# The head of a fused attention and MLP block: x tile 1 through ScalarE's queue, its statistics beside a square root, its transposes inside the first V group, tile 3 transposed by DMA

## Chip, cores, metric

One core of one Trainium2 chip. The metric is the device time of one execution in microseconds (us). "Before" and "changed" name the two kernels.

## The reference

A pre-normalized block: sliding-window attention, then a SiLU MLP, both with a residual, for one sequence of 2048 tokens with 1024 channels.

```python
h  = x + attention(layernorm(x), wqkv, wo)      # 32 heads of 32, window 256
h2 = h + silu(layernorm(h) @ w1) @ w2           # F = 3584
# x [1,2048,1024], wqkv [1024,3072], all bfloat16
# layernorm: (x - mean) / sqrt(var + 1e-5), no weights
```

Only the first 25 us matter here: the first 512 tokens ("block 0", four tiles of 128) are loaded, normalized, transposed, and multiplied by wv, then by the q and k columns of wqkv.

## The kernel before

The loads at the start, all from SP's queue (`wv` is the last third of wqkv, in two halves of 1 MB; each x tile has 256 KB):

```python
load_x(0, 0)
load_wqkv(2 * D)             # wv, first half
load_x(0, 1)
load_wqkv(2 * D + 512)       # wv, second half
load_x(0, 2)
load_x(0, 3)
for c0 in (0, D, 512, D + 512):
    load_wqkv(c0)            # q and k columns
```

Normalization of a tile and its transpose for block 0. VectorE takes the statistics, ScalarE the square root, TensorE transposes into PSUM, ScalarE copies to SBUF:

```python
def ln_first(xt, st, rs, j):
    ln_stats(xt, st, j)                                   # VectorE: 2 bn_stats, 1 bn_aggr
    nc.scalar.activation(out=rs[:, j:j + 1], in_=st[:, j, 1:2], func=ACT.Sqrt, bias=eps[:], scale=1.0)
    nc.vector.reciprocal(out=rs[:, j:j + 1], in_=rs[:, j:j + 1])
    for h in range(2):
        ln_norm(xt[:, h * 512:(h + 1) * 512], st, rs, j)  # VectorE

def turn_first(xt, dst, j):
    for h in range(2):
        ...                                               # four TensorE transposes
        nc.scalar.copy(...)                               # PSUM -> SBUF
```

The order of block 0. `v_group(0, j, c)` is eight matmuls of 128x128 by 128x512 for tile j and half c of wv; `qk_group` the same for 128 columns of q or k and all four tiles:

```python
ln_first(x_ring[0], st, rs, 0)
turn_first(x_ring[0], lnT_b[0], 0)
ln_first(x_ring[1], st, rs, 1)
v_group(0, 0, 0, act)
turn_first(x_ring[1], lnT_b[0], 1)
ln_first(x_ring[2], st, rs, 2)
v_group(0, 1, 0, act)
v_group(0, 0, 1, act)
turn_first(x_ring[2], lnT_b[0], 2)
ln_first(x_ring[3], st, rs, 3)
v_group(0, 1, 1, act)
v_group(0, 2, 0, act)
turn_first(x_ring[3], lnT_b[0], 3)
v_group(0, 2, 1, act)
dummy = small.tile([P, 1], F32, name="dummy", tag="dummy")   # pool "small": two buffers
nc.scalar.activation(out=dummy[:], in_=eps[:], func=ACT.Exp) # draws the table load forward
v_group(0, 3, 0, act)
v_group(0, 3, 1, act)
...
for g in range(G):                                           # G = 8
    qk_group(0, 0, g, act)
    qk_group(0, 1, g, dve)
    ...
```

The softmax here doesn't subtract the row's maximum and nothing guards it: scores larger than these inputs give would overflow.

## Time and profile before

| | before |
|---|---|
| time, median of 3 (range) | 698.12 us (698.09 to 698.29) |
| span of the profile | 696.4 us |
| TensorE busy | 99% |
| first q/k group starts in the chain | 24.22 us |

The chain of waits is read from the end of the program backwards; where it names TensorE without a break, only less TensorE work or an earlier start can shorten the time. The prediction shows its head, the timeline and the DMA rate.

### The profile page before, as it was taken

How to read it: one execution, taken by the hardware profiler on the slowest of the kernel's cores; microseconds unless marked ns; L12 is line 12 of the kernel's file. 1: busy time of each engine (PE TensorE's matmuls, PEld its weight loads, DVE VectorE, ACT ScalarE, POOL GpSimd, SP SyncE). 2: the span in 40 equal slices, each digit the busy share in tenths (PEclk: the TensorE clock that was granted, in tenths of full speed). 3: DMA queues.
4: the chain of work that ended last, by engine and by line, in shares of the span. 5: the costliest groups of instructions: out<-in, count | busy, mean ns of one | idle time of the engine just before them, and what ended most of it. 6: DMA issues, size and time to landing. Idle time of an engine off the chain costs nothing.

```text
span 696.4 us, 12339 instructions
## 1 busy us (share of the span) xinstructions
PE 690.6 (99%) x5099; PEld 332.1 (48%) x5099; DVE 288.1 (41%) x608; ACT 258.5 (37%) x323; POOL 175.2 (25%) x391
## 2 busy tenths in 40 slices
PE   8999999999999999999999999999999999999998
PEld 3444444555555555544444444444444444444445
DVE  5347645743444448543315234433133251233111
ACT  4316667777777777621310023300033200233000
POOL 1006676777777777600000000000000000000000
PEclk9999999999999999999999999999999999999999
DMA  9541142036331678891123510023300024100010
GB/s 312 171 65 66 25 86 68 17 54 176 92 122 24 190 257 262 203 315 40 32 75 99 106 38 1 1 78 81 84 0 1 10 94 93 45 1 1 30 39 24
DMA packets 75400, 60.57 MB, mean 87 GB/s; under 512 B 49232, under 2 KB 59472, under 8 KB 75344
## 3 DMA queue, kind: packets, MB, share of 16 engines
q1 hardware_dynamic: 75344, 59.78, 30.8%
q8 instruction: 40, 0.66, 0.4%
q14 instruction: 16, 0.13, 0.1%
HBM read 39.85 MB, written 8.39 MB: 69 GB/s over the span
## 4 chain that ended last, share of the span: by engine, by line
PE 98%; DMA 1%; DVE 0%; ACT 0%; SPq 0%; issue 0%
PE hacc L540 19%; PE hacc L577 17%; PE acc L240 16%; PE acc L577 10%; PE acc L540 9%; PE acc L230 8%; PE acc L259 7%; PE o_ps L331 4%; PE sc L277 3%; PE hacc L259 1%; PE o_ps L346 1%; PE sc L305 1%; DMA r_o<-in_A_x_dram 1%; PE o_ps L208 0%; DVE ln_st L170 0%; ACT r_w L209 0%
## 5 line engine op out<-in xcount | busy, mean ns | idle before, releaser
L322 POOL TENSOR_SCALAR_AFFINE_SELECT r_e<-r_e 128x256 bf16<-128x256 bf16 (+1 forms) x384 | 172.3, 479 | 116.7 <-ACT r_e L314 65.9
L285 ACT ACTIVATE r_e<-sc 128x1024 bf16<-128x1024 f32 x144 | 139.5, 1021 | 45.1 <-PE sc L277 31.0
L577 PEld LDWEIGHTS <-r_a 128*128 128x128 bf16 x952 | 90.9, 98 | 103.0
L540 PEld LDWEIGHTS <-r_w 128*128 128x128 bf16 x896 | 87.3, 98 | 104.8
L577 PE MATMUL hacc<-r_a 128*128 128x512 bf16 (+2 forms) x616 | 122.5, 360 | 0.0
L540 PE MATMUL hacc<-r_e,r_w 128*128 128x512 bf16 x456 | 100.9, 379 | 0.0
L549 ACT ACTIVATE r_n<-hacc 128x512 f32<-128x512 f32 x30 | 17.9, 597 | 178.9 <-PE hacc L540 178.9
L577 PE MATMUL acc<-r_a 128*128 128x512 bf16 x336 | 74.0, 379 | 0.0
L240 PEld LDWEIGHTS <-r_w 128*128 128x128 bf16 x512 | 46.5, 98 | 57.0 <-issue 7.0
L242 DVE CAST r_a<-acc 128x512 bf16<-128x512 f32 x56 | 38.7, 690 | 73.1 <-PE acc L240 56.5
L240 PE MATMUL acc<-r_t,r_w 128*128 128x512 bf16 x256 | 60.0, 379 | 0.0
L240 PE MATMUL acc<-r_w 128*128 128x512 bf16 x256 | 58.2, 380 | 0.0
L259 PE MATMUL acc<-r_o,r_a 128*128 128x512 bf16 x208 | 49.4, 380 | 0.0
L540 PE MATMUL acc<-r_e,r_w 128*128 128x512 bf16 x216 | 49.1, 379 | 0.0
L331 PEld LDWEIGHTS <-r_e 128*128 128x128 bf16 x1152 | 39.6, 96 | 17.0
L314 ACT ACTIVATE r_e<-sc 128x1024 bf16<-128x1024 f32 x36 | 34.9, 1021 | 21.2 <-PE sc L305 20.1
L331 PE MATMUL o_ps<-r_a,r_e 128*128 128x33 bf16 x1152 | 40.2, 178 | 0.0
L592 DVE SCALAR_TENSOR_TENSOR r_t<-hacc,r_t 128x512 bf16<-128x512 f32 (+2 forms) x22 | 14.0, 635 | 56.3 <-PE hacc L577 56.3
L259 PEld LDWEIGHTS <-r_a 128*128 128x128 bf16 x256 | 23.1, 98 | 29.6 <-issue 5.1
L592 DVE SCALAR_TENSOR_TENSOR r_t<-acc,r_t 128x512 bf16<-128x512 f32 x12 | 8.3, 692 | 64.2 <-PE acc L577 64.2
L550 DVE SCALAR_TENSOR_TENSOR r_a<-r_n,hacc 128x512 bf16<-128x512 f32 x30 | 20.6, 688 | 33.0 <-ACT r_n L549 33.0
L540 PE MATMUL hacc<-r_a,r_w 128*128 128x512 bf16 x144 | 32.9, 379 | 0.0
(70 smaller groups left out, 476.6 us busy)
## 6 DMA issues: line engine op xcount, KB each, us to landing
r_w<-in_B_w_dram SPq DMA_DIRECT2D x8, 896.0 KB, 5.5
r_a<-in_B_w_dram SPq DMA_DIRECT2D x7, 1024.0 KB, 8.7
r_w<-in_A_wqkv_dram SPq DMA_DIRECT2D x6, 1024.0 KB, 11.4
r_o<-in_A_x_dram SPq DMA_DIRECT2D x16, 256.0 KB, 3.6
h_dram<-r_t SPq DMA_DIRECT2D x16, 256.0 KB, 3.7
r_t<-h_dram SPq DMA_DIRECT2D x16, 256.0 KB, 2.8
out_dram<-r_t SPq DMA_DIRECT2D x31, 128.0 KB, 1.7
r_e<-h_dram SPq DMA_DIRECT2D x3, 1024.0 KB, 5.8
```

The source lines that it names most:

```text
L230: nc.tensor.matmul(acc, lhsT=lnT_b[b % 2][:, kt, j * P:(j + 1) * P], rhs=wv[:, kt, c * 512:(c + 1) * 512], start=(kt == 0), stop=(kt == KT ...
L240: nc.tensor.matmul(acc, lhsT=wqk[:, kt, col0:col0 + P], rhs=lnT_b[b % 2][:, kt, :], start=(kt == 0), stop=(kt == KT - 1))
L242: copy(out=(qT, kT)[which][b][:, g, :], in_=acc)
L259: nc.tensor.matmul(acc, lhsT=qT[b][:, g, j * P:(j + 1) * P], rhs=wo[:, g, c * 512:(c + 1) * 512], start=(g == 0), stop=(g == G - 1))
L277: nc.tensor.matmul(sc[hh // 2][:, hh % 2, ch * P:(ch + nq) * P], lhsT=kT[t // 4][r0:r0 + DH, g, (t % 4) * P:(t % 4 + 1) * P], rhs=qT[b][r0 ...
L285: nc.scalar.activation(out=e, in_=sc[pair], func=ACT.Exp, scale=scale)
L314: nc.scalar.activation(out=e, in_=sc[pair], func=ACT.Exp, scale=scale)
L322: nc.gpsimd.affine_select(out=ap, in_=ap, pattern=[[0, 2], [0, n], [sgn, P]], compare_op=ALU.is_ge if upper else ALU.is_gt, fill=0.0, base ...
L331: nc.tensor.matmul(o_ps[pair][:, qt * 2 + hh, 0:VW], lhsT=e_of(i, kind, pair)[:, hh, ch * P:(ch + 1) * P], rhs=v[:, b * 4 + kt, g * 4 + pa ...
L540: nc.tensor.matmul(acc, lhsT=w1[:, kt, ft * P:(ft + 1) * P], rhs=ln2T[b][:, kt, :], start=(kt == 0), stop=(kt == KT - 1))
L577: nc.tensor.matmul(acc[:, 0:c1 - c0], lhsT=gT[:, ft, j * P:(j + 1) * P], rhs=w2[ft // 4][:, ft % 4, c0:c1], start=(ft == 0), stop=(ft == F ...
L592: nc.vector.scalar_tensor_tensor(out=t_out[j % 2][:, c0:c1], in0=acc[:, 0:c1 - c0], scalar=0.5, in1=t_in[j % 2][:, c0:c1], op0=ALU.mult, o ...
```

## The change

The intent is to feed TensorE earlier and leave no holes in the first 24 us: x1 no longer stands behind 1 MB of weights, its statistics begin while ScalarE takes tile 0's square root, its transposes run between the matmuls of tile 0's first V group, and tile 3 is transposed by DMA. Three of the four q/k weight loads are held back behind that DMA transpose, so that it finds an empty queue, and the q/k groups are regrouped to need those weights later.

```diff
+    eps = const.tile([P, 1], F32, name="eps")
+    nc.vector.memset(eps[:], LN_EPS)
+    dummy = const.tile([P, 1], F32, name="dummy")
+    nc.scalar.activation(out=dummy[:], in_=eps[:], func=ACT.Sqrt)
+
     load_x(0, 0)
     load_wqkv(2 * D)
-    load_x(0, 1)
+    load_x(0, 1, nc.scalar)
     load_wqkv(2 * D + 512)
     load_x(0, 2)
     load_x(0, 3)
-    for c0 in (0, D, 512, D + 512):
-        load_wqkv(c0)
+    load_wqkv(0)
 ...
-    def ln_first(xt, st, rs, j):
-        ln_stats(xt, st, j)
+    def ln_first(xt, st, rs, j, half_done=None, ahead=None):
+        ln_stats(xt, st, j, half_done)
         nc.scalar.activation(out=rs[:, j:j + 1], ..., func=ACT.Sqrt, ...)
+        if ahead is not None:
+            ln_half(ahead[0], ahead[1], 0)
         nc.vector.reciprocal(out=rs[:, j:j + 1], in_=rs[:, j:j + 1])
 ...
-    ln_first(x_ring[0], st, rs, 0)
+    half = small.tile([P, 2, 6], F32, name="ln_st", tag="ln_st")
+    ln_first(x_ring[0], st, rs, 0, None, (x_ring[1], half))
     turn_first(x_ring[0], lnT_b[0], 0)
-    ln_first(x_ring[1], st, rs, 1)
-    v_group(0, 0, 0, act)
-    turn_first(x_ring[1], lnT_b[0], 1)
+    ln_first(x_ring[1], st, rs, 1, half)
+    def turn_1(kt):                                  # called before matmul kt
+        if kt in (5, 7):
+            turn_first(x_ring[1], lnT_b[0], 1, (kt // 2 - 2,))
+    v_group(0, 0, 0, act, turn_1)
 ...
     ln_first(x_ring[3], st, rs, 3)
+    ln_transpose(x_ring[3], lnT_b[0], 3)             # DMA transpose from SP
+    for c0 in (D, 512, D + 512):
+        load_wqkv(c0)
     v_group(0, 1, 1, act)
     v_group(0, 2, 0, act)
-    turn_first(x_ring[3], lnT_b[0], 3)
     v_group(0, 2, 1, act)
-    dummy = small.tile([P, 1], F32, name="dummy", tag="dummy")
 ...
-    for g in range(G):
-        qk_group(0, 0, g, act)
-        qk_group(0, 1, g, dve)
+    for g0 in range(0, G, 4):
+        for w in range(2):
+            for g in range(g0, g0 + 4):
+                qk_group(0, w, g, dve if g % 2 else act)
```

More of the change, by code (lines that the diff above doesn't have):

```diff
@@ L135, with load_x @@
     w2_v = B_w2.rearrange("(ft p) n -> p ft n", p=P)
-    def load_x(b, j):
-        nc.sync.dma_start(out=x_ring[(b % 2) * 4 + j], in_=x2d[(b * 4 + j) * P:(b * 4 + j + 1) * P, :])
+    def load_x(b, j, queue=nc.sync):
+        queue.dma_start(out=x_ring[(b % 2) * 4 + j], in_=x2d[(b * 4 + j) * P:(b * 4 + j + 1) * P, :])
     def load_wqkv(c0):
@@ L150 @@
     load_x(0, 3)
-    for c0 in (0, D, 512, D + 512):
-        load_wqkv(c0)
+    load_wqkv(0)
     ident = const.tile([P, P], BF16, name="ident")
     make_identity(nc, ident[:])
-    eps = const.tile([P, 1], F32, name="eps")
-    nc.vector.memset(eps[:], LN_EPS)
     warm = ebuf[0]
@@ L164, with ln_half, ln_stats @@
         nc.tensor.matmul(sc[0][:, i % 2, :], lhsT=warm[:, 0, 0:P], rhs=warm[:, 0, :], start=True, stop=True)
-    def ln_stats(xt, st, j):
-        stats = small.tile([P, 2, 6], F32, name="ln_st", tag="ln_st")
-        for c in range(2):
-            nc.vector.bn_stats(out=stats[:, c, :], in_=xt[:, c * 512:(c + 1) * 512])
+    def ln_half(xt, stats, c):
+        nc.vector.bn_stats(out=stats[:, c, :], in_=xt[:, c * 512:(c + 1) * 512])
+    def ln_stats(xt, st, j, half_done=None):
+        stats = half_done
+        if stats is None:
+            stats = small.tile([P, 2, 6], F32, name="ln_st", tag="ln_st")
+            ln_half(xt, stats, 0)
+        ln_half(xt, stats, 1)
         nc.vector.bn_aggr(out=st[:, j, :], in_=stats[:])
@@ L202, in ln_first, with turn_first @@
             ln_norm(xt[:, h * 512:(h + 1) * 512], st, rs, j)
-    def turn_first(xt, dst, j):
-        for h in range(2):
+    def turn_first(xt, dst, j, halves=(0, 1)):
+        for h in halves:
             for i in range(4):
@@ L228, in v_group @@
             if between:
-                between()
+                between(kt)
             nc.tensor.matmul(acc, lhsT=lnT_b[b % 2][:, kt, j * P:(j + 1) * P], rhs=wv[:, kt, c * 512:(c + 1) * 512],
@@ L238, in qk_group @@
             if between:
-                between()
+                between(kt)
             nc.tensor.matmul(acc, lhsT=wqk[:, kt, col0:col0 + P], rhs=lnT_b[b % 2][:, kt, :],
@@ L422 @@
     steps = sum(ln1_steps(1), [])
-    for g in range(G):
-        qk_group(0, 0, g, act)
-        qk_group(0, 1, g, dve)
-        for _ in range(2):
-            if steps:
-                steps.pop(0)()
+    for g0 in range(0, G, 4):
+        for w in range(2):
+            for g in range(g0, g0 + 4):
+                qk_group(0, w, g, dve if g % 2 else act)
+                n = g0 * 2 + w * 4 + g % 4
+                for _ in range(0 if n < 4 else 1 if n < 10 else 2):
+                    if steps:
+                        steps.pop(0)()
+    assert not steps
     def load_w1(kt):
@@ L438, with between @@
     count = [0, 0]
-    def between():
+    def between(kt):
         k, m = count
```

## The prediction

> **What bounds the kernel now.** I read the page first (engine shares, the chain that ended last), then the chain in order of time for the first 26 us, the timeline of the same stretch, and the one-microsecond windows for the DMA. The page says that TensorE is busy nearly all the time and that the chain is TensorE almost everywhere:
>
> ```profile
> PE 690.6 (99%) x5099; PEld 332.1 (48%) x5099; DVE 288.1 (41%) x608; ACT 258.5 (37%) x323; POOL 175.2 (25%) x391
> ...
> PE 98%; DMA 1%; DVE 0%; ACT 0%; SPq 0%; issue 0%
> ```
>
> So nothing outside the head can win more than crumbs, and the head is short. Its chain:
>
> ```profile
> 1.73 5.68 DMA r_o<-in_A_x_dram
> 7.41 0.02 issue
> 7.43 1.30 DVE ln_st L170 x2
> ...
> 9.99 0.41 PE o_ps L208 x4
> 10.40 0.02 issue
> 10.42 0.59 ACT r_w L209
> 11.02 0.05 issue
> 11.06 3.63 PE acc L230 x16
> 14.69 0.45 PE o_ps L208 x8
> 15.14 3.45 PE acc L230 x16
> 18.59 0.45 PE o_ps L208 x8
> 19.04 5.18 PE acc L230 x24
> 24.22 1.94 PE acc L240 x9
> ```
>
> The reader is to see three things. Up to 11.06 us the end is set by x tile 1: its load lands at 1.73 + 5.68 = 7.41, and its statistics, transposes (L208, eight of 128x128) and PSUM copies (L209) follow. From 11.06 us on TensorE runs without a gap: V groups (L230, eight matmuls, 1.73 us each by 3.45 us for 16), and two blocks of transposes of 0.45 us. The first q/k group (L240) starts at 24.22. That number is the one to follow: behind it TensorE takes 698.12 - 24.22 us whatever the head does, so each tenth that the q/k start moves should show in the total. (The span of the profile is 696.4, the timed run 698.12; I carry differences over, not levels.)
>
> The first V group ran before this chain, from 7.32 us, and there TensorE does have holes:
>
> ```profile
> 7.32 1.90 PE L230 MATMUL acc<-r_w 128*128 128x512 bf16 x8 [0.36 <-ACT r_w L209]
> ...
> 9.99 0.72 PE L208 MATMUL o_ps<-ident,r_o 128*128 128x128 bf16 x8 [0.77 <-DVE r_o L191]
> ```
>
> 0.77 us idle before tile 1's transposes, and 0.35 us before the next V group while ScalarE copies. Between 7.32 and 24.22 (16.90 us) eight V groups need 8 x 1.73 = 13.8 us; the other 3.1 us are three blocks of transposes and these holes. This is all that the change can attack. The DMA side of the head, in the windows (last columns: DMA share, GB/s):
>
> ```profile
> 4.00:5.00 1.00, 1.00 (x4) 0.36 (x3) 0.97 (x2) 0.00 (x0) 0.00 (x0) 1.00 1.09 383
> ...
> 10.00:11.00 1.00, 0.71 (x8) 0.44 (x8) 0.26 (x1) 0.58 (x2) 0.00 (x0) 1.00 1.05 382
> ```
>
> From 3 us on the DMA engines are full, at 345 to 383 GB/s. The loads land in the order of their issue (start plus time to landing, by small windows on the two issuing lines): x0 at 3.7, first half of wv at 6.66, x1 at 7.41, second half of wv at 10.4, x2 at 11.1, x3 at 4.2 + 7.6 = 11.8, the first q/k weights at 14.7. An order can be swapped; the sum of bytes ahead of x2 (256 KB x 3 plus 2 MB) can't be.
>
> **What the Trainium skill says.** (1) "DMA: Bandwidth & Descriptors", section "Issuing engines are not separate DMA queues": transfers started by different engines run on the same 16 DMA engines and interleave. The full windows above agree with its consequence: a second queue brings no bandwidth, it only lets x1 share with the wv half that it stood behind. No run yet shows two queues. (2) "Perfetto Trace Analysis", section "Per-engine timelines": a ScalarE instruction is pushed into a wait queue and the sequencer goes on decoding. By that, x1's issue need not wait for the table load and the dummy square root ahead of it; the kernel before issues nothing from ScalarE, so its trace can't say. (3) "ScalarE: Activation LUTs", section "What ACT_TABLE_LOAD costs": 1283 ns for the load and a drain of about 1380 ns. The trace has 1.28 us for the load at 0.80 and again at 21.41, but the dummy after the latter starts at 22.70, straight away: no drain shows. The first load is already hidden (0.80 to 2.08, first needed at 5.25), so drawing the square root's load forward by a dummy wins nothing.
>
> **Part by part.**
> *x1 on ScalarE's queue.* If it is issued near 1.2 us (between two of SP's issues of 0.4 us each), its data starts while x0's still flows. x0's bytes moved at about 350 GB/s from some 2.0 to 2.75 us; sharing from 2.4 on makes x0 land about 0.3 later, near 3.95 instead of 3.69, and x1 near 4.7 instead of 7.41. The wv half takes x1's place, near 7.4. All are estimates from the windows.
> *Half of tile 1's statistics beside the square root of tile 0.* One half is 0.65 us (1.29 for two, L170). VectorE's gap there is 0.36 us (5.22 to 5.58: square root 0.29 and its hand-overs), so the reciprocal of tile 0 comes 0.3 us later. With x0's 0.27 the first V group moves from 7.32 to about 7.9. That is a loss on tile 0, bought for tile 1: second half 7.05 to 7.7, aggregate to 7.94, but its square root stands in ScalarE's order behind tile 0's two PSUM copies (2 x 0.59, until 8.4): 8.4 to 8.65, reciprocal, first half normalized for TensorE at about 9.35.
> *Transposes of tile 1 inside the first V group.* Matmuls kt 0 to 4 fill 7.9 to 8.97, then 0.38 us of waiting for 9.35, four transposes (0.23), kt 5 and 6, four more, kt 7: group over near 10.5. Tile 1's first copy ends at 10.4, so the second V group starts at 10.5 without a hole, against 11.06. Gain so far: 0.56 us, of it 0.35 the copy's hole.
> *Tile 2.* Two V groups take until 13.95. Tile 2's load lands at 11.1 as before, so its chain is untouched: its normalization starts at 13.19 and TensorE can transpose from about 13.65. So no wait, and the fourth V group starts near 14.4 rather than 15.14 in the chain (14.97 in the timeline). Gain 0.55 to 0.7 us.
> *Tile 3 by DMA.* It removes eight transposes (0.45 us of TensorE) and two ScalarE copies. Three V groups then run 14.4 to 19.6. But tile 3 must be there: statistics 13.85 to 15.13 on VectorE (behind tile 2's), aggregate 15.37, square root behind the V copy and tile 2's two copies on ScalarE (until about 15.6): 15.9, normalized by 16.85. The issue-to-landing time of such a transpose is seen at 42.70 us (3.4 us alone), with a median of 3.2 and up to 4.8 for the whole trace. 16.9 + 3.3 = 20.2. So the seventh V group waits 0.6 us, which eats the 0.45 that was saved and a little more. Two V groups later q/k starts at 20.25 + 3.45 = 23.7. Against 24.22: 0.5 us.
> *q/k weights later, q/k order regrouped.* The change holds three weight loads behind the transpose, so that it finds empty queues; from 18.2 us they land 3 us apart, near 23, 26 and 29. Regrouped, the second is first needed four groups (6.9 us) after 23.7, the third after eight: hidden, with 7 us to spare. x tiles of the next block land near 31; VectorE's first copy behind them (group 5, due at 34) is safe by 3 us. The 16 steps end at group 14 instead of the eighth pair; block 1's first transpose lands near 49, needed at 51: safe. Copies alternate between ScalarE and VectorE as before, so a group stays 1.73 us. Worth 0.
>
> Sum: first groups +0.55, tile 2 +0.1, tile 3 +0.45 less 0.6 of waiting: **0.5 us less, 697.6 us**.
>
> **The rivals.** *The DMA transpose is slow or early.* If it lands in 3.1 us and ScalarE's square root comes at 15.4, the landing is 19.8 and q/k starts at 23.3: 697.2. If it takes 4.8 us as the slowest did, landing is 21.7, q/k at 25.1: 699.0. For the first speaks that the queues are then empty (the first q/k weights land at 14.7); the 4.8 us came in a stretch with other transposes. *x1's issue waits for the table load.* Then it leaves at 2.3, lands near 5.8, and the half statistics in VectorE's order hold up tile 0's reciprocal until 6.45: first V group at 8.2 to 8.3, fourth at 14.7. Tile 3's chain hides most of it: 23.8, 697.7. *x0 and x1 share so badly that both land at 4.7.* First V group at 8.6: two thirds of the gain gone, 697.9. *The best case:* tile 2 (13.65) bounds, and tile 3 is ready: q/k at 22.9, 696.8. Against it stands the sum of tile 3's chain. *A late weight or x tile stalls q/k:* margins of 3 and 7 us speak against it.
>
> **Range and chances.** TensorE's path is fixed to some 0.1 us (three runs within 0.2), so the width comes from the end of tile 3's transpose: 19.6 to 21 us, that is 697.0 to 698.4. I put the low end slightly lower for a head that lands better than I reckon: 696.9 to 698.4. 2% is 14 us, more than half of the whole head: within 2% with 0.98, one in a hundred for either side.
>
> **What would show it.** In the changed kernel's timeline: x1 issued from ScalarE before 1.7 us and statistics of tile 0 starting at 3.9 to 4.1; one 0.65 us statistic between tile 0's aggregate and reciprocal; first V group at 7.7 to 8.1, fourth near 14.4; the two V groups of tile 3 waiting for a DMA 0.3 to 1 us, near 20.2; first q/k matmul at 23.7, and no wait of TensorE from there to the scores at 51. The prediction is wrong if the V groups of tile 3 don't wait at all (then the gain is about 1 us), or if q/k starts later than 24.2, or if the q/k groups of the first block take more than 27.7 us.

## The result, and the profile after

| | before | changed |
|---|---|---|
| time, median of 6 (range) | 698.21 us (698.09 to 698.37) | 697.06 us (696.83 to 697.44) |
| ratio (95% interval) | | 0.9984 (0.9971 to 0.9997) |
| span of the profile | 696.4 us | 694.9 us |

1.15 us less: inside the predicted range of 696.9 to 698.4. But it is twice the predicted 0.5 us, and the spread of the six runs has doubled. The page of the changed kernel, engine shares and chain:

```profile
PE 684.8 (99%) x5004; PEld 331.4 (48%) x5091; DVE 288.2 (41%) x608; ACT 257.5 (37%) x322; POOL 174.5 (25%) x391
...
PE 98%; issue 1%; DVE 0%; DMA 0%; ACT 0%
```

As before, TensorE is all of it. (Some matmul records are missing from this trace, 5004 against 5091 weight loads, so its busy sum isn't compared.) The chain in order of time, changed kernel (start, us, what; L239 is now the V group, L217 the transposes, L249 the q/k groups):

```profile
0.81 2.86 DMA r_o<-in_A_x_dram
...
5.22 0.56 DVE ln_st L170
...
9.80 3.24 PE acc L239 x15
...
13.47 0.45 PE o_ps L217 x8
13.91 5.18 PE acc L239 x24
19.09 0.03 issue
19.13 3.63 PE acc L239 x16
22.75 0.22 PE acc L249
```

The chain now starts with x0, not x1, passes through the half statistic (5.22), and is TensorE alone from 9.80 instead of 11.06. The q/k groups start at 22.75 instead of 24.22: 1.47 us earlier, which is the difference of the spans, 1.5. The wait for tile 3's transpose, predicted at 0.6 us, is in the chain only as the 0.03 at 19.09, but it is longer. The chain counts the matmul before the wait up to its own end, 0.38 us after its start, while matmuls in a row start 0.216 us apart (3.45 us for 16). The timeline of TensorE, in two narrow windows, has the starts:

```profile
18.28 0.81 PE L239 MATMUL acc<-r_w 128*128 128x512 bf16 x3
...
19.13 0.39 PE L239 MATMUL acc<-r_w 128*128 128x512 bf16 x1
```

The next matmul could have started at 18.28 + 3 x 0.216 = 18.93. It started at 19.13, 0.05 us after the transpose had landed (19.08, by the trace). So TensorE waited 0.2 us, a third of what was predicted. The timeline of the same stretch, changed kernel:

```profile
0.97 0.38 ACTq L139 DMA_DIRECT2D r_o<-in_A_x_dram  x1
...
5.13 0.64 DVE L170 BATCH_NORM_STATS2 ln_st<-r_o 128x6 f32<-128x512 bf16 x1
...
5.69 0.15 DVE L209 RECIPROCAL rs_a<-rs_a 128x1 f32<-128x1 f32 x1
...
7.42 1.25 PE L239 MATMUL acc<-r_w 128*128 128x512 bf16 x5 [0.35 <-ACT r_w L218]
...
10.58 1.29 DVE L170 BATCH_NORM_STATS2 ln_st<-r_o 128x6 f32<-128x512 bf16 x2 [1.57 <-DMA r_o<-in_A_x_dram]
...
16.25 1.34 SPq L202 DMA_TRANSPOSE r_w<-r_o  x1
```

x1 is issued at 0.97 us, while the table load (0.80 to 2.08) still runs. Tile 2 is used from 10.58, not 11.10. And the DMA windows of 7 to 12 us (last two columns: DMA share, GB/s) hold a surprise. First before, then changed:

```profile
7.00:12.00 5.00, 3.56 (x21) 1.62 (x22) 3.30 (x8) 2.69 (x6) 0.00 (x0) 1.00 1.08 360
```

```profile
7.00:12.00 5.00, 4.57 (x28) 2.11 (x27) 2.70 (x8) 2.70 (x6) 0.00 (x0) 1.00 1.08 392
```

The engines are full in both, yet the changed kernel moves 9% more. Even transposes that the change never touched are quicker, hundreds of microseconds later. The page's DMA issues (last column: median us from issue to landing), before and changed:

```profile
r_e<-r_e SPq DMA_TRANSPOSE x12, 3.2
```

```profile
r_e<-r_e SPq DMA_TRANSPOSE x12, 2.7
```

Nothing in the prediction, and nothing in the stated intent, speeds up a DMA.

### The profile page after: what moved, and what is told of

Same layout as the page of the kernel before. It is cut to its first block, busy times and chain, and to the rows that moved or that the text cites. A ratio compares the mean times of both kernels' runs of the same rounds, so it can differ in the third digit from the quotient of the medians.

```text
span 694.9 us, 12233 instructions
## 1 busy us (share of the span) xinstructions
PE 684.8 (99%) x5004; PEld 331.4 (48%) x5091; DVE 288.2 (41%) x608; ACT 257.5 (37%) x322; POOL 174.5 (25%) x391
## 4 chain that ended last, share of the span: by engine, by line
PE 98%; issue 1%; DVE 0%; DMA 0%; ACT 0%
PE hacc L558 18%; PE hacc L595 17%; PE acc L249 16%; PE acc L595 10%; PE acc L558 9%; PE acc L239 8%; PE acc L268 7%; PE o_ps L340 4%; PE sc L286 3%; PE hacc L268 1%; PE o_ps L355 1%; PE sc L314 1%; DMA r_o<-in_A_x_dram 0%; DVE ln_st L170 0%; PE o_ps L217 0%
## 5 line engine op out<-in xcount | busy, mean ns | idle before, releaser
L249 PEld LDWEIGHTS <-r_w 128*128 128x128 bf16 x512 | 46.5, 98 | 57.0 <-issue 7.0
L249 PE MATMUL acc<-r_t,r_w 128*128 128x512 bf16 x241 | 58.5, 380 | 0.8
L249 PE MATMUL acc<-r_w 128*128 128x512 bf16 x245 | 57.6, 380 | 0.6
```

The costliest lines, as they stand in the source:

```text
L249: nc.tensor.matmul(acc, lhsT=wqk[:, kt, col0:col0 + P], rhs=lnT_b[b % 2][:, kt, :], start=(kt == 0), stop=(kt == KT - 1))
```

## The experiments

Four theories came up. **A**: the schedule does it all, and the DMA rate is the state of one chip or one run. **B**: the second queue or the new order raises the rate. **C**: the change moved the large SBUF tiles by accident, and their start sets the rate. **D**: x1 beside x0 delays x0 and with it the whole head, by a varying amount.

One measure serves throughout. "First stat" is when VectorE starts tile 0's statistics, that is, when x0 has landed; "q/k" is when the chain enters the q/k groups. Their difference takes out x0's arrival, which varies from run to run. That holds where the chain begins with x0, as in the changed kernel, again_after, tile3_pe, no_ahead, tiles23_dma and both_early. In the others it begins with another load (x1 in the three traces of the kernel before without a second queue, in x1_later and in both; the first half of wv in x1_sp_first and x1_act_alone; x2 in after_shifted); there a late x0 makes the difference smaller without any gain, and the q/k column is the one to read. All runs were on one chip but those marked with a star: the first two are the traces of the two kernels above, the last ran on another chip.

| run | median us (range) | first stat | q/k | difference |
|---|---|---|---|---|
| before* | 698.12 | 3.69 | 24.22 | 20.53 |
| changed* | 697.06 (696.83 to 697.44) | 3.69 | 22.75 | 19.06 |
| same_chip_before | 698.07 (one run) | 3.65 | 24.12 | 20.47 |
| again_after | 697.24 (696.95 to 697.51) | 4.06 | 23.11 | 19.05 |
| x1_sp_first | 698.29 (697.81 to 699.31) | 3.56 | 25.20 | 21.64 |
| tile3_pe | 697.22 (697.03 to 697.55) | 3.88 | 23.18 | 19.30 |
| before_aligned | 698.02 (697.76 to 698.44) | 3.90 | 24.26 | 20.36 |
| after_shifted | 698.02 (697.74 to 698.14) | 4.17 | 23.95 | 19.78 |
| x1_act_alone | 698.27 (698.14 to 698.35) | 4.28 | 24.14 | 19.86 |
| tiles23_dma | 697.13 (697.08 to 698.29) | 3.64 | 22.14 | 18.50 |
| x1_later | 699.63 (698.94 to 701.08) | 3.67 | 26.94 | 23.27 |
| both | 697.97 (697.01 to 700.06) | 3.65 | 25.92 | 22.27 |
| no_ahead | 697.24 (697.09 to 697.46) | 3.88 | 23.16 | 19.28 |
| both_early* | 696.69 (696.54 to 697.26) | 3.77 | 22.19 | 18.42 |

The kernel before had a median of 698.16 to 698.18 in the rounds on the one chip, and 698.07 beside both_early. From q/k to the end of the span all runs but one take 672.1 to 672.4 us (before 696.4 - 24.22, after_shifted 696.2 - 23.95, both_early 694.6 - 22.19): the head alone moves the time, as the prediction assumed. The one is tiles23_dma with 673.1: its last row of matmuls starts 0.33 us before the changed kernel's (685.45 and 685.78), yet its span is 0.3 us longer, so the end behind the matmuls varies too. A single trace shows the structure; the rounds have the weight for the time.

### same_chip_before and again_after

Both kernels unchanged, on one chip.

> The kernel before, unchanged, for its profile on the chip on which the changed kernel is profiled too. Theory A (part of the 1.44 us by which the q/k start moved in the two traces is the DMA's state in the one trace, not the change): beside the changed kernel on one chip the head's DMA rate is the same within 3%, either some 350 GB/s in both or some 385 in both, and x tile 2 lands within 0.2 us of the same time in both. Theory B (a second queue raises the rate): here again 345 to 365 GB/s and x2 at 11.1, the changed kernel 380 to 400 and x2 at 10.6.

> The changed kernel, unchanged, beside the kernel before on the same chip. Theory A: about 1.1 us less than before (ratio 0.9984), the q/k start between 22.7 and 23.3; if the DMA is slow here (x2 at 11.1), the head waits for tile 2 and for tile 3's transpose as was predicted. Theory B: q/k start at 22.8 again, whatever the kernel before shows.

Measured: 359 GB/s from 7 to 12 us before and 391 changed, tile 2 used from 10.98 and 10.79. The changed kernel is 0.92 us below the 698.16 of its rounds, ratio 0.9986 (0.9973 to 1.0000). So the rate belongs to the program, and theory A falls in the form "state of the chip". Something in the change makes the DMA faster. Also, x0 was first used at 4.06 here and at 3.69 in the other trace of the same kernel.

### x1_sp_first

```diff
     load_x(0, 0)
+    load_x(0, 1)
     load_wqkv(2 * D)
-    load_x(0, 1, nc.scalar)
```

> The changed kernel with x tile 1 issued from SP, between x0 and the first half of wv, instead of from ScalarE. Theory A (only the order counts; the queue gains nothing but issue time): within 0.15 us of the changed kernel; x1 lands near 4.5, wv's half near 7.4, the first V group starts at 7.4 to 7.6. Theory B (the second queue carries more): DMA rate back to 350 GB/s, x2 at 11.1, time 0.4 to 0.6 us above the changed kernel.

Measured: 698.29, the whole gain lost, but not for either reason. From 7 to 12 us the rate was 385 GB/s with a single queue, so theory B's second queue is out as its cause. Instead the first half of wv landed late, at 1.73 + 6.74 = 8.47 by the chain, and the first V group waited for it. In the changed kernel it landed at 1.26 + 5.9 = 7.16; of the 1.31 us between them, 0.47 are its later issue. The timeline, and two windows (last three columns: granted clock of TensorE, DMA share, GB/s), of this run:

```profile
8.51 2.29 PE L239 MATMUL acc<-r_w 128*128 128x512 bf16 x5 [1.57 <-DMA r_w<-in_A_wqkv_dram]
```

```profile
4.00:5.00 1.00, 1.00 (x4) 0.35 (x3) 0.97 (x3) 0.00 (x0) 0.00 (x0) 1.00 0.81 161
9.00:10.00 1.00, 1.00 (x4) 0.33 (x3) 0.00 (x0) 0.00 (x0) 0.00 (x0) 0.50 1.10 392
```

From 4 to 5 us the DMA moved only 161 GB/s at a share of 0.81, and behind the pause of TensorE the granted clock was 0.50 from 8.5 to 11.5 us. The profiled run is the slowest of the five (699.31), but the fastest was 697.81, still above every run of the changed kernel. So the queue does matter, in a way that no theory had: with x1 issued second on SP's queue, the weights came late in this one trace, the slowest run. Why the rate sinks there stays open.

### tile3_pe

```diff
     ln_first(x_ring[3], st, rs, 3)
-    ln_transpose(x_ring[3], lnT_b[0], 3)
     ...
     v_group(0, 2, 0, act)
+    turn_first(x_ring[3], lnT_b[0], 3)
     v_group(0, 2, 1, act)
```

> The changed kernel with tile 3 transposed by TensorE and copied by ScalarE where the kernel before did it (weights still held back). Theory A: eight transposes back on a gapless TensorE, 0.45 us more than the changed kernel. Rival (the DMA transpose only swaps TensorE time for a wait, as the prediction had it): the same time within 0.15 us.

Measured: 697.22 against 697.24, the same. The chain of this run has the transposes back:

```profile
14.10 3.45 PE acc L239 x16
17.56 0.45 PE o_ps L217 x8
18.00 3.67 PE acc L239 x17
```

From the fourth V group to q/k it takes 23.18 - 14.10 = 9.08 us, the changed kernel 22.75 - 13.91 = 8.84. So the DMA transpose saves 0.45 us of TensorE, and the 0.2 us of waiting for its landing take part of that back. (The 3.63 us that the chain gives the sixteen matmuls of tile 3, instead of 3.45, are no slower matmuls: 15 starts 0.216 us apart and the last one's 0.38 make 3.62.) The net is 0.25 us in the traces, too little to show in the medians. The rival, "it only swaps TensorE time for a wait", is half right: about half of the time saved goes into the wait.

### before_aligned and after_shifted: 32 bytes

What do all changed kernels share, x1_sp_first too? In the kernel before, `dummy` came from a pool with two buffers, 2 x 32 bytes per partition; the change takes it from the pool of constants, one slot of 32 bytes. In the built programs every large tile therefore starts 32 bytes lower: `r_w` at byte 17,408 of the partition instead of 17,440. The first is a multiple of 512, the second lies 32 bytes past one. Two runs test this both ways. In the kernel before, one tile moves pool:

```diff
     nc.vector.memset(eps[:], LN_EPS)
+    dummy = const.tile([P, 1], F32, name="dummy")
     ...
-    dummy = small.tile([P, 1], F32, name="dummy", tag="dummy")
```

> The kernel before with one line moved: the 4-byte tile dummy comes from the pool of constants (one slot of 32 bytes) instead of the double-buffered one (two slots), as in the change; all large SBUF tiles then start 32 bytes lower, on a multiple of 512 bytes (17,408 instead of 17,440 for r_w). Theory C (the change moved the tiles onto an aligned start by accident, and that sets the DMA rate): 385 to 395 GB/s from 7 to 12 us instead of 360, x tile 1 landing near 7.1 instead of 7.3 to 7.4, q/k start near 23.8, time some 0.3 us less. Rival B (the rate comes from the new order or the second queue): 360 GB/s and 698.15, unchanged.

In the changed kernel, a pad puts the tiles back:

```diff
     dummy = const.tile([P, 1], F32, name="dummy")
+    pad = const.tile([P, 1], F32, name="pad")
+    nc.vector.memset(pad[:], 0.0)
```

> The changed kernel with another 32-byte tile among the constants, so that the large tiles start at 17,440 as in the kernel before; one more memset of 0.06 us on an idle VectorE. Theory C: 350 to 360 GB/s, x tile 2 near 11.1, tile 3's transpose 3.2 us, V groups of tile 3 waiting about 0.6 us, q/k start near 23.7, time 697.6 to 697.7: what the prediction had. Rival B: 390 GB/s and 697.2, as the changed kernel.

Measured, the windows of before_aligned and of after_shifted:

```profile
7.00:12.00 5.00, 3.79 (x26) 1.68 (x24) 3.53 (x8) 3.03 (x6) 0.00 (x0) 1.00 1.08 391
```

```profile
7.00:12.00 5.00, 4.57 (x32) 2.19 (x30) 2.30 (x7) 2.93 (x6) 0.00 (x0) 1.00 1.08 359
```

The rate follows the 32 bytes in both kernels: 360 before, 391 before with the move, 391 to 392 changed, 359 changed with the pad. The other runs agree: x1_act_alone at 17,440 has 359; tile3_pe, no_ahead and x1_later at 17,408 have 391 or 392. The transposes of r_e take 2.8 us in before_aligned and 3.2 in after_shifted. So theory C holds for the rate, and B is dead. Only these two starts were tried, so which boundary counts (17,408 is a multiple of 64, 128 and 256 too) is not shown. The times are where it becomes interesting, and there the expectations missed. Aligned, the kernel before gains 0.15 us (698.02 against 698.17, ratio 0.9997, 0.9984 to 1.0011: no clear difference), and its q/k start of 24.26 is no earlier than before: x1, which bounds it, was used from 7.47, not 7.1. Shifted, the changed kernel loses 0.78 (698.02 against 697.24; no run of one overlaps the other) and is left with 0.15 of its gain (ratio to before 0.9996, 0.9982 to 1.0009: no clear difference either); 697.6 to 697.7 had been expected. Each of the two, the schedule and the tile start, is worth about 0.15 us alone, together about 0.9. The chain of after_shifted says why:

```profile
2.34 9.13 DMA r_o<-in_A_x_dram
...
17.08 3.19 DMA r_w<-r_o
...
20.32 3.63 PE acc L241 x16
23.95 0.22 PE acc L251
```

The chain begins with x2's load, and tile 3's transpose stands in it with 3.19 us. Beside again_after, the changed kernel on the same chip, x2 was used from 11.49 us instead of 10.79. Tile 3's transpose was issued at 17.08 instead of 16.62, 0.46 us later, and took 3.19 us instead of 2.81, 0.38 more. So it landed 0.84 us later, and q/k started 0.84 us later (23.95 and 23.11): about the 0.78 us of the medians. In the kernel before neither counts: x2 comes while TensorE is still busy, and tile 3 is not transposed by DMA. The new schedule moved x2 and a DMA transpose onto the path, and only then does the DMA's rate count.

### x1_act_alone

The kernel before, at the old tile start, with only x1's queue changed (and the dummy square root; `eps` moves up for it, and the old `dummy` line goes).

```diff
+    dummy = const.tile([P, 1], F32, name="dummy")
+    pad = const.tile([P, 1], F32, name="pad")          # keeps r_w at 17,440
+    nc.vector.memset(pad[:], 0.0)
+    nc.scalar.activation(out=dummy[:], in_=eps[:], func=ACT.Sqrt)
     ...
-    load_x(0, 1)
+    load_x(0, 1, nc.scalar)
```

> The kernel before with x tile 1 issued from ScalarE behind a dummy square root, nothing else, and the large tiles kept at 17,440 by a pad: one part alone at the old alignment. x1 lands at 4.3 to 4.6 instead of 7.4, tile 1's chain runs behind tile 0's and ScalarE's copies, transposes of tile 1 near 9.4, second V group near 10.4 instead of 11.06, q/k start near 23.6: time 0.6 us less than before, if the sum of the prediction holds. Rival (tile 2 at 11.1 takes the gain back): 0.3 us less.

Measured: 698.27, no gain at all, against 0.6 us expected and 0.3 by the rival. Timeline:

```profile
4.28 1.29 DVE L175 BATCH_NORM_STATS2 ln_st<-r_o 128x6 f32<-128x512 bf16 x2 [2.76 <-DMA r_o<-in_A_x_dram]
...
7.93 1.89 PE L235 MATMUL acc<-r_w 128*128 128x512 bf16 x8 [0.37 <-DMA r_w<-in_A_wqkv_dram]
```

The first V group starts at 7.93 instead of 7.32, 0.61 us later, and two things hold it there at once. x0 was used only from 4.28 (tile 0's first PSUM copy ended at 7.87), and the first half of wv, behind x1 now, landed at 1.27 + 6.62 = 7.89 instead of 6.66; the chain names the weights. By these landings an x0 in time would not have helped. The second V group starts at 10.99 instead of 11.06, and q/k at 24.14 instead of 24.22: what the earlier x1 gains, the later loads of x0 and wv lose.

Over the runs with x1 issued from ScalarE at 0.97 us the first stat lies at 3.69, 4.06, 3.88, 4.17, 4.28, 3.64, 3.88 and 3.77, mean 3.92; where x1 leaves later or from SP it is 3.69, 3.65, 3.56, 3.90, 3.67 and 3.65, mean 3.69. That fits theory D, with 0.23 us on average, and a scatter that fits the wider spread of the changed kernel's runs. It isn't shown: each is one trace, the two ranges overlap, and the tile start is mixed in (the two runs at 17,440 have the 4.17 and the 4.28; the six at 17,408 have a mean of 3.82).

### no_ahead

```diff
-    ln_first(x_ring[0], st, rs, 0, None, (x_ring[1], half))
+    ln_first(x_ring[0], st, rs, 0)
+    ln_half(x_ring[1], half, 0)
```

> The changed kernel without statistics of tile 1 beside the square root: both halves after tile 0's normalization. By the trace of the changed kernel the half costs tile 0 0.11 us (reciprocal 0.68 us after the aggregate's start instead of 0.57), and its absence puts 0.65 us into tile 1's chain, of which ScalarE's two copies hide 0.3 or so. From the first statistic to the q/k start 19.2 to 19.4 us instead of 19.05: 0.2 us more in the time, at the edge of what the rounds resolve. Rival (tile 2's arrival bounds anyway): 19.05, no difference.

Measured: 19.28 us from first stat to q/k, as expected; the median of 697.24 shows nothing of it (x0's scatter is as large). The half statistic beside the square root is worth 0.2 us in the trace, no more.

### x1_later

If x1 beside x0 is the trouble, let it leave later: a memset of two of its columns makes ScalarE's issue wait.

```diff
-    load_x(0, 1, nc.scalar)
     ...
     nc.vector.memset(warm, 0.0)
+    nc.vector.memset(x_ring[1][:, 0:2], 0.0)
+    load_x(0, 1, nc.scalar)
```

> The changed kernel with x tile 1 still issued from ScalarE, but behind a two-column memset of its buffer on VectorE, so near 1.6 us instead of 0.97. Theory D (x1 sharing the engines with x0 delays x0 by 0 to 0.5 us from run to run, and the whole head with it: x0 used from 3.69 and 4.06 in the two traces of the changed kernel): statistics of tile 0 start at 3.6 to 3.75, x1 still lands by 5.1, q/k start at 22.7 to 22.9, median 696.9 and a spread under 0.4. Rival (x1 now lands after 5.1 and the half statistics hold up tile 0): q/k start at 23.1 or later, 697.2 or more.

Measured: 699.63, 1.5 us worse than the kernel before. The profiled run is the slowest of five (701.08), and the first run of the kernel before in these rounds was slow too (700.79), so the trace may show more than the edit does; but the fastest run, 698.94, is still above the median before. x0 came in time (3.67), but x1 did not. Timeline and a window of this run:

```profile
1.55 0.38 ACTq L139 DMA_DIRECT2D r_o<-in_A_x_dram  x1
...
6.85 0.69 DVE L171 BATCH_NORM_STATS2 ln_st<-r_o 128x6 f32<-128x512 bf16 x1 [1.65 <-DMA r_o<-in_A_x_dram]
```

```profile
10.00:11.00 1.00, 1.00 (x4) 0.30 (x2) 0.91 (x4) 0.03 (x1) 0.00 (x0) 0.50 1.04 387
```

Issued 0.29 us behind the wv half (1.26), x1 needed 5.3 us, hardly less than the 1 MB (which landed at 1.26 + 6.3). Issued 0.29 us ahead of it, 3.4 us. Now the half statistic, which stands in VectorE's order ahead of tile 0's reciprocal, holds up tile 0 by 1.8 us (reciprocal at 7.46 instead of 5.69); TensorE stands still from 5.4 to 8.1, and its granted clock is 0.50 from 8 to 14 us. The rival is right, and stronger than it was put.

### tiles23_dma, both, both_early: a better version

First step, against the changed kernel: tile 2 by DMA too, x2 and x3 ahead of the second wv half, all q/k weights behind the two transposes.

```diff
-    load_wqkv(2 * D + 512)
     load_x(0, 2)
     load_x(0, 3)
-    load_wqkv(0)
+    load_wqkv(2 * D + 512)
     ...
-    turn_first(x_ring[2], lnT_b[0], 2)
+    ln_transpose(x_ring[2], lnT_b[0], 2)
     ...
-    for c0 in (D, 512, D + 512):
+    for c0 in (0, D, 512, D + 512):
```

> The changed kernel with tile 2 transposed by DMA as well, x tiles 2 and 3 loaded ahead of the second half of wv and all q/k weights behind the two transposes. Eight transposes less on TensorE (0.45 us) and no wait for tile 2: if x2 lands near 7.5 its transpose is issued near 12 and lands near 15, just when the fifth V group needs it: q/k start 22.3 to 22.7, time 0.3 to 0.5 us below the changed kernel. Rival (the second half of wv lands too late behind x2 and x3, or the transposes wait for it): no gain or a loss of 0.3 us.

Measured: 697.13, 0.11 below the changed kernel's median, where 0.3 to 0.5 were expected. q/k started at 22.14, somewhat earlier than expected; the end behind it was 0.7 to 1 us longer. The 56 matmuls of seven V groups run without a gap, but the chain shows where the gain stops:

```profile
16.52 5.58 DMA r_w<-in_A_wqkv_dram
...
22.14 2.12 PE acc L248 x9
```

q/k waits for its first weights, which left only behind the second transpose. So half of them go ahead, together with the late x1 (against tiles23_dma; the issue of x1 as in x1_later isn't repeated):

```diff
     load_wqkv(2 * D + 512)
+    load_wqkv(0, 256)                 # first 256 columns of q
     ...
+    load_wqkv(256, 256)
-    for c0 in (0, D, 512, D + 512):
+    for c0 in (D, 512, D + 512):
```

> A try at a better version: x1 as in the run before, tiles 2 and 3 by DMA, x2 and x3 ahead of the second half of wv, the first 256 columns of the q weights loaded ahead of the two transposes and the rest behind them. If tile 2's transpose is not held up by the half megabyte ahead of it, the V groups run without a gap to 21.8 and q/k starts there: 696.0 to 696.3. Rival (the transpose waits for that load): fifth V group 0.5 us late, 696.6 to 696.9.

Measured: 697.97, above both ranges expected, with three runs at 697.01 to 697.16 and three at 698.78 to 700.06. In the trace, which is of the slowest, the late x1 spoils it (half statistic at 7.48), as in x1_later. But V and q/k follow each other without a gap in its chain. So x1 goes back to 0.97 us:

> The last try at a better version: tiles 2 and 3 by DMA with half of the first q weights ahead of the two transposes, x tile 1 issued from ScalarE at 0.97 us again (the delayed issue cost 1.6 us and more, for x1 then landed at 6.9 to 7.5 behind the wv half). In the run with tiles 2 and 3 by DMA q/k waited for its weights until 22.14 us, 18.5 us after tile 0's first statistic; in the run of both no gap stood between the V groups and q/k. If that holds here, q/k starts 18.2 us after the first statistic, 21.8 to 22.3, time 696.1 to 696.6, that is 0.6 to 1.1 us below the changed kernel. Rival (the transpose of tile 2 waits behind the half megabyte): 18.7 us or more after the first statistic, 697.0.

Measured: 696.69 (696.54 to 697.26), 1.38 us below the kernel before in its rounds (698.07), ratio 0.9981 (0.9968 to 0.9995).

```profile
13.18 9.01 PE acc L239 x41
22.19 1.94 PE acc L249 x9
```

No wait stands between the V groups and q/k. It ran on another chip than the other runs, and never beside the changed kernel: against the kernel before of its own rounds it gains 1.38 us, the changed kernel 1.15 and 0.92. It is the fastest here by those figures, though its intervals against before overlap with those of the changed kernel (0.9968 to 0.9995; 0.9971 to 0.9997). The time is just above the expected 696.1 to 696.6; q/k came 18.42 us after the first stat, against an expected 18.2.

## Why the prediction was right, and where it was not

The time fell into the range, in part by luck. The centre, 697.6 against 697.06 and 697.24, came out 0.4 to 0.5 us too high, because a term was missing that no line of the diff announces. Without that term, in after_shifted, the schedule gained 0.15 us and not the forecast 0.5; with it 0.92 to 1.15. So two errors, one each way, stand behind a number that fitted.

The prediction had named this outcome and argued against it: "the best case", tile 2 bounding and tile 3 ready, q/k at 22.9, 696.8. Measured were 22.75 and 23.11. It had also said that it would be wrong if the V groups of tile 3 don't wait at all, with a gain of about 1 us. They waited 0.2 us, less than the 0.3 to 1 that it gave as its sign of being right, and the gain was about 1 us: by its own signs that step failed.

**What bounds the kernel, and that q/k's start carries the time over.** Right: 672.1 to 672.4 us behind q/k in all runs but one.

**x1 leaves before the table load ends; x1 delays x0.** Right. The issue was at 0.97 us, while the table load ran until 2.08 (the Trainium skill's "Perfetto Trace Analysis", "Per-engine timelines", agrees: the sequencer goes on decoding). The delay of x0, estimated at 0.27, was 0.23 on average over single traces (not shown, see x1_act_alone), with a scatter of 0 to 0.6 that the prediction did not foresee. Its rival of a sharing so bad that x0 lands at 4.7 did not come.

**The half statistic costs tile 0 0.3 us.** Mis-sized: 0.11 (2.00 us from first stat to reciprocal against 1.89). It starts at 5.13 under the end of the aggregate, not at 5.25 with the square root.

**The second V group without a hole.** Right, and earlier than reckoned. ScalarE took tile 1's square root 0.32 us after the first V group's start (7.74 and 7.42), not 0.45 to 0.5.

**"Tile 2's load lands at 11.1 as before, so its chain is untouched."** This step failed: 10.58 and 10.79. The sum of bytes ahead of x2 was indeed the same; the rate was not, and the step took the rate as given. With the rate put back (after_shifted) x2 was used from 11.49, later than the prediction's 11.1, and stood at the head of the chain.

**"So the seventh V group waits 0.6 us, which eats the 0.45 that was saved."** This step failed too, by the same cause: the transpose took 2.8 us instead of 3.3 and was issued at 16.25 and 16.62 instead of 16.9. The wait was 0.2 us. In after_shifted it came back: TensorE could have gone on at 19.58 + 0.216 = 19.80 and started at 20.32, a wait of 0.53 us. There the transpose was issued at 17.08 and landed at 20.27, where the prediction had 16.9 and 20.2. So at the old tile start the step is described well; what the prediction missed is the alignment, 0.84 us of q/k start between after_shifted and again_after, 0.78 us of time. The gain at the old tile start was over-estimated all the same: q/k came at 23.95, not 23.7.

**The weights, the q/k order and the next block worth nothing.** No wait of TensorE appears there in the trace; not tested by a run of its own, like the transposes inside the V group.

What stays open: why two x tiles in a row on SP's queue make the weights late (x1_sp_first), and by what path in the DMA 32 bytes cost 8% of the rate.

## What to carry to other kernels

A schedule that takes the slack out of a head puts DMA latencies onto the path, so first look at what sets them: here the start of the big tiles within a partition, which a 4-byte scratch tile shifted, decided whether the rest of the change paid. When a profile shows speed-ups in work that the change does not touch, stop explaining by the diff and look for a side effect; padding one kernel and un-padding the other settles it in two runs. And measure a step from the event that feeds it (here first stat to q/k), for the arrival of a load can scatter more than the step is worth; but look in the chain first whether that event feeds it in this run. Last, a chain that ends a row of matmuls at the last one's own end hides part of a wait: compare starts.

## What the Trainium skill lacked or had wrong

- "DMA: Bandwidth & Descriptors", "How a descriptor splits into AXI transactions": the page says that the first transaction of a descriptor which does not start on a 256-byte boundary starts at the boundary below, and the bytes before the start, fetched but unused, still cost beats of the bus. It gives no measured rate. Here the SBUF side 32 bytes off a 512-byte boundary (and so off a 256-byte one) gave 359 to 360 GB/s, on it 391 to 392, and DMA transposes of r_e 3.2 against 2.7 to 2.8 us. No run shows that the splitting is the cause. No page warns that a pool of small tiles shifts the large ones.
- The same page, "Queues, rings and completion order": each DMA engine is said to go round the queues that have work, packet by packet. Here x1 (256 KB), issued 0.29 us behind 1 MB on the other queue, landed 5.3 us after its issue, nearly with the megabyte; issued 0.29 us ahead, after 3.4 us. Equal shares from x0's landing on (3.67 us) would have taken about 1.4 us for twice 256 KB at the 385 GB/s measured, an estimate, so x1 would have landed near 5.1 and not at 6.83. The page counts packets in descriptors (typically 9 to 17), so equal shares of bytes are an assumption of this document, and no run tests the rule.
- The same page, "Issuing engines are not separate DMA queues", says that a second issuing engine only saves the time of the issue. The rate agrees (385 GB/s with one queue, 391 with two, from 7 to 12 us), but moving x1 to SP's queue ahead of the weights cost 1.05 us (698.29 against 697.24), and the later issue of the weights (1.73 instead of 1.26 us, 0.47) explains less than half of it. The rest stays open.
- "TensorE: Matmul & The Clock Gate", "What's actually happening", gives at least one idle window of about 3.4 us for the fall to half clock. Here shorter pauses were followed by a granted clock of 0.50: 1.57 us before the first V group of x1_sp_first (0.50 from 8.5 to 11.5 us; 0.72 us of transposes and 0.40 us of idling lie before that pause), and 2.71 us in x1_later (0.50 from 8 to 14 us). No run varied the pause by itself.
